# Two more attention heads transposed by VectorE and DRAM, and the plan of the late heads shifted to match, in a fused attention and two-layer feed-forward kernel

## The chip, the cores and the metric

The kernel runs on one core of one Trainium2 chip. The metric is device time in microseconds (us) of one execution, lower is better. A run is shown as the median of several executions; one further execution is recorded by the hardware profiler.

## The reference

Causal attention with a forget gate, then two feed-forward networks, all in float32:

```python
# attention: batch 4, 8 heads, 576 tokens, head width 64  (32 heads in all)
decay  = cum[..., :, None] - cum[..., None, :]       # cum = cumsum(log(clip(f)))
scores = where(causal, -1e9, q @ k.T / 8 + decay)
attn   = softmax(scores)                             # with 1e-9 in the denominator
x      = concat_heads(attn @ v)                      # 2304 tokens x 512
h = maximum(x @ w_in, 0);  x = (h * h) @ w_out       # 512 -> 2048 -> 512
h = x @ w_in2;  out = (h - tanh(h)) @ w_out2         # 512 -> 2048 -> 512
```

## The kernel before

Every operand of a product is kept as a rounded high part and a low rest, and a product is three passes on TensorE (high x high, low x high, high x low).

The first feed-forward runs in 8 blocks `j` of 288 tokens, each of 16 steps `i` over the hidden width: `h_step` (12 products `hp`, L168), then relu and two squares on ScalarE, the low part `gl` on GpSimd or VectorE, and two steps later `y_step` (12 products `yp`, L197). The 32 attention heads are worked beside these steps, so that their results are there when block `j` needs them. The second feed-forward (L1203, L1279) follows and is not touched.

There are three forms of attention work:

- `first_a` and `first_b`: heads 0 to 7, in two parts; `first_a` runs ahead of the first step and also splits the first weights of the feed-forward into high and low parts (`weights_early`, with `split_a` and `split_b`, at the head-steps that `SPLIT_A` and `SPLIT_B` give).
- `attention`: heads 8 to `UT - 1`. The softmax P is transposed by TensorE (`trans`, L549, 15 transposes a head into `t_ps`), and copied from PSUM as high (ScalarE) and low (VectorE). A generator yields after each piece; `advance` asks for pieces, so many by each half-step: 40 pieces of `first_b` and `F0` more by half-step `ENDS[0]` of block 0, the rest by half-step `ENDS[1]` of block 1.
- planned heads: `UT` to 31. P is turned in 32 x 32 blocks by VectorE (`turn`, L564 to L570), stored to DRAM (`put`, four DMAs, L574), and loaded with its blocks in their places (`get`, four DMAs into `PTl`, L580). ScalarE then makes the high part `PTh` (`p_high`), VectorE the low one (`p_low`), and `pv_begin` and `pv_end` issue the products `o_ps` (L609, L614). `plan_head` puts each of these calls into a slot; a slot is a half-step, counted from block 2 on, so that block 1 has the slots -32 to -1. Head `k` begins in slot `o = START + int(PERIOD * (k - UT - 1))`. In the blocks 2 to 5 the calls of a slot that are planned `behind` come after the step's `hp` or `yp` products, the others ahead of them.

Puts, gets, stores of x (`store_x`, L497 and L498) and loads of q, k, v and of x go through SP's queue, in the order in which they are emitted. In `pv_parts`, `out` (slot o + 7) ends with `store_x` for every second head, whose low part GpSimd makes.

The program's instructions are emitted in the order of the source. Up to the step `MARK` (block, step) the order on each engine is that of the compiler framework's scheduler; behind it, that of emission. `tc.issue_after(ins)` holds the instructions of a block behind `ins` on its engine. The letters of `ENG` name the engine of an operation (V VectorE, A ScalarE, P GpSimd, S SP's queue).

Of the kernel before, what the change touches and what calls it, by code (L numbers as in the profile page):

```python
# [16 lines left out]
B, H, S, D = 4, 8, 576, 64  # L17
# [8 lines left out]
LAG = 2  # L26
RING = 3
XLOADS = (((8, 0, 4),), ((11, 0, 3), (13, 3, 4)), ((13, 0, 4),))
F0 = 18
SLK = (None, 8)  # L30
MARK = (2, 0)
BUSY = (34, 2, 4, 6, 4, 0, 0, 0)
UT = 16
ENDS = (28, 26)
PERIOD = 7.75
START = -4
ENG = {
# [7 lines left out]
}  # L45
FETCH = {6: 4, 7: 5, 8: 6}
SPLIT_A = {4: 0, 6: 1, 8: 2, 9: 3}
SPLIT_B = {5: 0, 7: 1, 9: 2, 10: 3}
EARLY_SPLIT = 4
AHEAD_W = 3  # L50
W2EARLY = 6
TB = 288
# [17 lines left out]
def kernel(  # L70
# [31 lines left out]
    def pre(u):  # L102
        return "" if u < UT else "l_"

    def by(name):
        return {"A": nc.scalar, "V": nc.vector, "P": nc.gpsimd, "S": nc.sync}[ENG[name]]
# [15 lines left out]
    def rest(eng, out, in_, hi):  # L122
        eng.tensor_tensor(out, in_, hi.bitcast(F32), ALU.subtract)  # L123
# [15 lines left out]
    def split_a(w, i, s, stage, tag, bufs):  # L139
        raw = RAW[i][:, s]  # L140
        tmp = stage.tile([128, 2, 512], F32, tag=tag, bufs=bufs, name="wst")
        x, t = tmp[:, 0], tmp[:, 1]
        if w.dtype == I64:
            raw = raw.rearrange("p (n c) -> p n c", c=2)
            tu = t.bitcast(U32)
            nc.scalar.activation(x, raw[:, :, 1].bitcast(F32), AF.Prelu, scale=2.0 ** -112, alpha=2.0 ** 32)
            by("w1_sh").tensor_scalar(tu, raw[:, :, 0], 29, None, ALU.logical_shift_right)
            nc.vector.scalar_tensor_tensor(tu, x.bitcast(U32), 3, tu, ALU.logical_shift_left, ALU.bitwise_or)
        else:
            rounded(nc.vector, t, raw[:, :512])  # L150
        STG[i, s] = t

    def split_b(i, s):
        t = STG.pop((i, s))
        if s == 0:
            HL[0] = slot_pool(i).tile([128, 2, 2, 512], F32R, tag=f"w{i}", name=f"w{i}")
        hl = W[1, i, s] = HL[0][:, s]
        rounded(nc.scalar, hl[:, 0], t)
        rest(by(f"w1_lo{s}"), hl[:, 1], t, hl[:, 0])
# [42 lines left out]
    two = att.enter_context(tc.tile_pool(name="two", bufs=2))  # L202
# [4 lines left out]
    R, QA, QB, VR, VH, ST, XS, P, PT = {}, {}, {}, {}, {}, {}, {}, {}, {}  # L207

    def latest(engine):
        return next(x for x in reversed(nc.cur_bb.bb.instructions) if x.engine == engine)  # L210
# [118 lines left out]
    def first(h, part):  # L329
# [76 lines left out]
        def o_step():  # L406
            ps = bank0(part, "o_ps")
            t0 = tiles[0]
            for c in ((0, 2, 3, 4, 1) if part else (0, 2, 1)):
                if c == 4:  # L410
                    nc.tensor.matmul(ps[0:64, 128:256], vr[0:64, 4], ptr[0][:, 0:128], start=False, stop=False)
                    continue
                t = max(t0, c)
                nc.tensor.matmul(ps[0:64, (t - t0) * 128:256], vr[:, c], pt[0][:, c, t - 1:t0 + 1].rearrange("p t j -> p (t j)"),  # L414
                                 start=(c == 0), stop=(c == 1))
            if not part:
                ps0 = bank0(part, "o0_ps")
                nc.tensor.matmul(ps0[0:64, 0:64], vr[0:64, 0], ptr[0][:, 0:64], start=True, stop=True)
            e = h % 2
            if e == 0:  # L420
                XS[0] = two.tile([128, S], F32, tag="xs", name="xs")
            xs = XS[0]
            rr = slice(64 * e, 64 * e + 64)
            c0 = 320 if part else 64
            rounded(by("b_xs" if part else "a_xs"), xs[rr, c0:c0 + 256], ps[0:64, 0:256])
            if not part:
                rounded(by("a_xs0"), xs[rr, 0:64], ps0[0:64, 0:64])
            if e == 1:
                if part:
                    store_x(0, h // 2, xs, 320, S)  # L430
                else:
                    rounded(nc.scalar, X[0][0][:, h // 2], xs[:, :TB])
                    rest(by("a_xl"), X[0][1][:, h // 2], xs[:, :TB], X[0][0][:, h // 2])
                    rounded(nc.scalar, XE[:, 0, h // 2].bitcast(F32R), xs[:, TB:320])
                    rest(nc.gpsimd, XE[:, 1, h // 2], xs[:, TB:320], XE[:, 0, h // 2])
                    if h == H - 1:
                        for a in range(2):
                            nc.sync.dma_start(x_d[0][:, :, a, TB:320].rearrange("k p n -> p k n"), XE[:, a])
# [316 lines left out]
    def plan(slot, f, *a, behind=False):  # L755
        PLAN.setdefault(slot, ([], []))[behind].append((f, a))

    def plan_head(k):
        o = START + int(PERIOD * (k - UT - 1))
        new, old = k < NU, k > UT  # L760
        if new:
            plan(o, s_products, k, 4, behind=True)
            plan(o + 1, s_min, k, 4)
            plan(o + 1, s_exp, k, 4)
            plan(o + 1, s_products, k, 3, behind=True)
            plan(o + 2, s_min, k, 3)
            plan(o + 2, s_exp, k, 3)
            plan(o + 2, s_products, k, 2, behind=True)
            plan(o + 2, s_products, k, 1, behind=True)
            plan(o + 3, s_min, k, 2)  # L770
            plan(o + 3, s_exp, k, 2)
            plan(o + 3, s_min, k, 1)
            plan(o + 3, s_min, k, 0)
            plan(o + 3, s_exp, k, 1)
            plan(o + 3, s_exp, k, 0)
            plan(o + 3, s_sum, k, 3, 5)
            plan(o + 3, s_norm, k, 4)
            plan(o + 3, s_norm, k, 3)
            plan(o + 4, turn, 4)
            plan(o + 4, s_sum, k, 0, 3)  # L780
            plan(o + 4, s_norm, k, 2)
            plan(o + 4, s_norm, k, 1)
            plan(o + 4, s_norm, k, 0)
            plan(o + 4, turn, 3)
        if old:
            plan(o + 4, p_high, 0)
            plan(o + 4, p_high, 1)
            plan(o + 4, p_high, 2)
            plan(o + 4, p_high, 3)
            plan(o + 4, p_low, 0)  # L790
            for c in (1, 2, 3):
                plan(o + 5, p_low, c)
            plan(o + 5, pv_begin, k - 1, behind=True)
            plan(o + 6, pv_end, k - 1, behind=True)
            plan(o + 7, lambda u: PV[u][2](), k - 1)
            plan(o + 7, lambda u: PV.pop(u)[3](), k - 1)
        if new:
            plan(o + 5, turn, 2)
            plan(o + 5, turn, 1)
            plan(o + 5, turn, 0)  # L800
            plan(o + 5, put, k)
            plan(o + 6, get, k, behind=True)
        if k == UT + 1:
            plan(o, prep_v, UT)
        if k + 1 < NU:
            if k > UT + 1:
                plan(o, load, k + 1)
            plan(o + 5, prep_hi_qk, k + 1)
            plan(o + 6, prep_copy, k + 1)
            plan(o + 6, prep_low, k + 1)  # L810
        if new:
            plan(o + 4, load_v, k)
            plan(o + 8, prep_v, k)
# [6 lines left out]
    X = {0: [f1.tile([128, NK, TB], F32R, tag="xhl", bufs=4, name="xhl") for _ in range(2)]}  # L820
    setup()

    def weights_early(h):
        if h in FETCH:
            fetch_w(w1, FETCH[h], FETCH[h])
        if h in SPLIT_B:
            for s in range(2):
                split_b(SPLIT_B[h], s)
        if h in SPLIT_A:
            for s in range(2):  # L830
                split_a(w1, SPLIT_A[h], s, two, "QA", 2)

    TA = one.tile([128, 2048], F32, tag="T", name="TA")
    XE = TA[:, 1024:1280].rearrange("p (a k n) -> p a k n", a=2, k=NK)
    first_a(weights_early)

    def w1_ahead(i):
        if EARLY_SPLIT <= i + AHEAD_W - 1 < NF:
# [21 lines left out]
    def advance(to):  # L860
        while cnt[0] < min(to, total):
            next(ga, None)
            PEI[cnt[0]] = latest(EngineType.PE)
            cnt[0] += 1
# [232 lines left out]
    later = []  # L1097
    for k in range(UT + 1, NU + 1):
        plan_head(k)
    for g in range(NB * NF + LAG):  # L1100
        j, i = divmod(g, NF)
        if (j, i) == MARK:
# [330 lines left out]
    for n in range(REST):  # L1433
        k, g = divmod(n, NG)
# [103 lines left out]
```

## Time and profile before

| | |
|---|---|
| median of 3 runs | 1002.09 us (1002.01 to 1003.88) |
| the profiled execution, its own time | 1002.52 us |
| its span, first to last instruction | 1000.7 us |
| TensorE busy, products and weight loads | 978.0 and 930.1 us |
| VectorE, ScalarE, GpSimd busy | 722.6, 615.8, 393.7 us |
| mean granted TensorE clock | 0.994 |

The span is what the views of the trace divide; what lies between it and the execution's own time is outside all instructions. Products overlap in the records, each is listed with its whole passage, so the distance between two starts tells what one costs. The steps of block 0 start at 48.9 us, of block 1 at 164.8, of block 2 at 262.6, of block 3 at 329.4, of block 4 at 395.9, of block 5 at 462.7, of block 6 at 523.2 and of block 7 at 574.3 us.

### The profile page before, as it was taken

The page shows a single profiled execution, that of the slowest core. Times are in us where ns is not written, and L with a number is a line of the kernel's source. Part 1 is how long each engine was busy: PE and PEld are TensorE (multiplying, and loading weights), DVE is VectorE, ACT ScalarE, POOL GpSimd, SP SyncE. Part 2 cuts the span into 40 slices and gives each one's busy share as a digit, 9 for nine tenths or more (in the row PEclk, how much of TensorE's full clock was granted, in tenths as well). Part 3 has the DMA queues.
Part 4 walks back from the last instruction along what each step waited for, and adds up shares of the span by engine and source line. Part 5 has one row for each costly group of instructions (what it writes and reads, how often), then busy time and mean ns, then how long its engine had stood idle before and what let it go on. Part 6 is the DMA issues. An engine that isn't in the chain of part 4 may idle for free.

```text
span 1000.7 us, 19994 instructions
## 1 busy us (share of the span) xinstructions
PE 978.0 (98%) x7144; PEld 930.1 (93%) x7144; DVE 722.6 (72%) x1715; ACT 615.8 (62%) x1387; POOL 393.7 (39%) x452
## 2 busy tenths in 40 slices
PE   7989999999999999999999999999999999999998
PEld 6767778888999999999999999999999999999998
DVE  5998774777676878778626577567878787887851
ACT  5988786766686777777657777455566553333330
POOL 4343565455454435454304547146657520000000
PEclk8999999999999999999999999999999999999999
DMA  8646551223657576766547984987776798434351
GB/s 259 256 129 207 174 164 65 92 83 122 202 204 251 205 235 221 248 217 225 195 161 265 348 284 175 396 335 265 273 269 240 252 349 330 148 117 137 127 169 64
DMA packets 91443, 211.56 MB, mean 211 GB/s; under 512 B 9208, under 2 KB 33840, under 8 KB 89040
## 3 DMA queue, kind: packets, MB, share of 16 engines
q1 hardware_dynamic: 91216, 210.29, 60.7%
q8 instruction: 56, 0.92, 0.4%
q14 instruction: 43, 0.35, 0.1%
q10 hardware_dynamic: 128, 0.01, 0.0%
HBM read 132.20 MB, written 78.05 MB: 210 GB/s over the span
## 4 chain that ended last, share of the span: by engine, by line
PE 82%; DVE 6%; DMA 5%; ACT 3%; issue 1%; POOL 1%; SPq 1%; DVEq 0%; POOLq 0%; ACTq 0%
PE yp L197 19%; PE hp L168 19%; PE wp L1279 16%; PE wp L1203 12%; PE o_ps L609 4%; PE wp L1291 2%; DMA g_d<-gq 2%; PE o_ps L414 2%; PE s_ps L373 1%; PE s_ps L702 1%; DVE wt L973 1%; PE s_ps L701 1%; PE t_ps L549 1%; DMA R<-in_qk_dram 1%; PE t_ps L395 1%
## 5 line engine op out<-in xcount | busy, mean ns | idle before, releaser
L168 PE MATMUL hp<-xhl,w 128*128 128x288 f32 x1536 | 234.6, 298 | 3.5 <-ACT xhl L110 1.6
L168 PEld LDWEIGHTS hp<-xhl,w 128*128 128x128 f32 x1536 | 212.6, 189 | 6.8 <-ACT xhl L110 1.8
L197 PE MATMUL yp<-gh,w 128*128 128x288 f32 x1024 | 213.1, 299 | 0.0
L197 PEld LDWEIGHTS yp<-gh,w 128*128 128x128 f32 x1024 | 165.1, 189 | 1.9 <-issue 1.3
L1203 PE MATMUL wp<-xo,wg 128*128 128x288 f32 x1152 | 160.2, 296 | 2.9 <-DVE gq L1210 2.7
L1279 PE MATMUL wp<-go,wg 128*128 128x256 f32 x1344 | 161.4, 283 | 0.0
L1279 PEld LDWEIGHTS wp<-go,wg 128*128 128x128 f32 x1344 | 161.4, 192 | 0.0
L1203 PEld LDWEIGHTS wp<-xo,wg 128*128 128x128 f32 x1152 | 155.5, 189 | 4.2 <-DVE gq L1210 4.1
L197 PE MATMUL yp<-gl,w 128*128 128x288 f32 x512 | 152.2, 297 | 0.6 <-POOL gl L123 0.6
L525 POOL TENSOR_SCALAR P<-P,ST 128x192 f32<-128x192 f32 (+4 forms) x120 | 96.6, 812 | 134.7 <-DVE ST L717 79.3
L110 ACT ACTIVATE go<-gt 128x1792 fp32r<-128x1792 f32 (+1 forms) x34 | 58.3, 1717 | 101.4 <-PE wp L1279 73.3
L514 ACT ACTIVATE P<-P,ST 128x320 f32<-128x320 f32 (+4 forms) x151 | 84.8, 562 | 38.2 <-DVE ST L505 37.8
L505 DVE CUSTOM_DVE_ANT_0 P<-s_ps,mk 128x320 f32<-128x320 f32 (+3 forms) x151 | 63.3, 436 | 61.2 <-PE s_ps L702 33.3
L123 DVE TENSOR_TENSOR gl<-tmp,gh 128x288 fp32r<-128x288 f32 x96 | 60.1, 627 | 53.2 <-ACT tmp L178 52.7
L197 PEld LDWEIGHTS yp<-gl,w 128*128 128x128 f32 x512 | 96.7, 189 | 1.2 <-POOL gl L123 0.8
L123 DVE TENSOR_TENSOR go<-gt,go 128x1792 fp32r<-128x1792 f32 (+1 forms) x34 | 69.6, 2047 | 35.4 <-ACT go L110 32.3
L174 ACT ACTIVATE tmp<-hp 128x288 f32<-128x288 f32 x128 | 51.7, 404 | 58.6 <-PE hp L168 56.5
L123 POOL TENSOR_TENSOR wt<-wt,whi 128x512 f32<-128x512 f32 (+1 forms) x48 | 60.6, 1283 | 59.2 <-ACT whi L110 27.6
L178 ACT ACTIVATE tmp<-tmp 128x288 f32<-128x288 f32 x128 | 56.7, 443 | 3.3
L177 ACT ACTIVATE gh<-tmp 128x288 fp32r<-128x288 f32 x128 | 56.1, 438 | 2.0
L1210 DVE TENSOR_TENSOR gq<-wp,sm 128x288 f32<-128x288 f32 x96 | 40.7, 452 | 17.6 <-ACT sm L1209 10.7
L1341 POOL TENSOR_TENSOR gq<-sm,sm 128x288 f32<-128x288 f32 x32 | 28.6, 893 | 56.0 <-ACT sm L1340 34.8
(167 smaller groups left out, 1720.3 us busy)
## 6 DMA issues: line engine op xcount, KB each, us to landing
wg<-wg_d SPq DMA_DIRECT2D x24, 896.0 KB
g_d<-gq SPq DMA_DIRECT2D x32, 576.0 KB
raw<-in_w_dram SPq DMA_DIRECT2D x16, 1024.0 KB
p_d<-T SPq DMA_DIRECT2D x64, 256.0 KB
PTl<-p_d SPq DMA_DIRECT2D x64, 256.0 KB
raw<-in_w_dram SPq DMA_DIRECT2D x32, 512.0 KB
gt<-g_d SPq DMA_DIRECT2D x32, 512.0 KB
R<-in_qk_dram SPq DMA_DIRECT2D x24, 576.0 KB
```

Source lines behind the costliest of these rows:

```text
L110: eng.activation(out, in_, AF.Copy)
L123: eng.tensor_tensor(out, in_, hi.bitcast(F32), ALU.subtract)
L168: nc.tensor.matmul(ps, w[:, k * 128:(k + 1) * 128], x[:, k], start=(jj == 0), stop=(jj == 11))
L174: nc.scalar.activation(tmp, ps, AF.Relu)
L177: nc.scalar.activation(gh, tmp, AF.Square)
L178: nc.scalar.activation(tmp, tmp, AF.Square)
L197: nc.tensor.matmul(yp[m][:, :n], w[:, c], x, start=(at == 0 and j == 0), stop=(at == NF - 1 and j == 2))
L505: nc.vector.tensor_tensor_reduce(p[:rows, a:b], ps[:rows, :b - a], mk[:rows, o:o + b - a], -0.125, 3.0e38 if mn is None else mn, ALU.add, ...
L514: nc.scalar.activation(p[:rows, :n], p[:rows, :n], AF.Exp, bias=mn, scale=-1.0, accum_out=st[:rows, 1, t:t + 1])
L525: by(n_by).tensor_scalar(p[:rows, :n], p[:rows, :n], st[:rows, 3, t:t + 1], 1.0, ALU.mult, ALU.mult)
L1203: nc.tensor.matmul(ps, wg[:, ws, k * 128:(k + 1) * 128], xo[:, xs, k], start=(i == 0 and first_), stop=(i == 5), skip_group_check=True)
L1279: nc.tensor.matmul(ps, wg[:, ws, m * 128:(m + 1) * 128], YO[n][xs][:, YX[xn]], start=(j == 0 and m == 0 and i == 0), stop=(j == 2 and i == ...
```

## The change

`UT` goes from 16 to 14: heads 14 and 15 leave `attention` and become planned heads. The plan starts at slot -20 instead of -4, now with head 15 (16 slots are two periods of 7.75 and a half). So block 0 takes 26 pieces beyond the 40 instead of 18, and block 1 the remaining 32 by half-step 13 instead of 58 by half-step 26. `MARK` moves to block 1, step 10. The loads `get` go from slot o + 6, behind, to slot o + 7, and there they stand behind `out` and its `store_x`. In the opening, the split of weight 3 moves one head-step later, its instructions of the last two head-steps are held behind ScalarE's latest instruction, and the low part of the last pair of x goes from GpSimd to VectorE (`a_xe`). Two pieces of `first_b` are asked for ahead of the first step.

```diff
-F0 = 18
+F0 = 26
-MARK = (2, 0)
+MARK = (1, 10)
-UT = 16
-ENDS = (28, 26)
+UT = 14
+ENDS = (28, 13)
-START = -4
+START = -20
     "a_xl": "P",
+    "a_xe": "V",
-SPLIT_A = {4: 0, 6: 1, 8: 2, 9: 3}
-SPLIT_B = {5: 0, 7: 1, 9: 2, 10: 3}
+SPLIT_A = {4: 0, 6: 1, 8: 2, 10: 3}
+SPLIT_B = {5: 0, 7: 1, 9: 2, 11: 3}
-  rest(by("a_xl"), X[0][1][:, h // 2], xs[:, :TB], X[0][0][:, h // 2])
+  rest(by("a_xl" if h < H - 1 else "a_xe"), X[0][1][:, h // 2], xs[:, :TB], X[0][0][:, h // 2])
             plan(o + 5, put, k)
-            plan(o + 6, get, k, behind=True)
+            plan(o + 7, get, k)
     def weights_early(h):
         if h in FETCH:
             fetch_w(w1, FETCH[h], FETCH[h])
+        with tc.issue_after(latest(EngineType.Activation)) if h == H + 2 else ExitStack():
             (split_b and split_a of SPLIT_B and SPLIT_A, as before)
     first_a(weights_early)
+    with tc.issue_after(latest(EngineType.Activation)):
+        weights_early(H + 3)
     for k in range(UT + 1, NU + 1):
         plan_head(k)
+    advance(2)
```

## Rows read from the trace of the kernel before

**Rows 1.** The table of stretches: length, busy us (instructions) of each engine, clock, DMA.

```profile
48.90:164.80 115.90, 108.73 (x641) 84.80 (x640) 90.32 (x246) 89.76 (x210) 56.86 (x76) 0.99 0.49 155
164.80:262.60 97.80, 97.33 (x658) 86.92 (x657) 67.21 (x228) 64.68 (x171) 52.30 (x72) 1.00 0.33 110
...
329.40:395.90 66.50, 66.50 (x491) 65.37 (x490) 54.51 (x142) 49.37 (x123) 32.04 (x37) 1.00 0.64 216
...
523.20:574.30 51.10, 51.10 (x385) 51.10 (x385) 31.68 (x58) 36.55 (x81) 24.00 (x20) 1.00 0.83 299
```

**Rows 2.** Waits of TensorE: us in total, times, longest.

```profile
PE hp L168 <- ACT xhl L110: 1.6, 1, 1.6
PE hp L168 <- DMA xhl<-x_d: 0.8, 1, 0.8
PE hp L168 <- POOL xhl L123: 0.6, 1, 0.6
```

**Rows 3.** The stretches again, products on o_ps alone (PE first).

```profile
164.80:262.60 97.80, 21.90 (x91) 13.32 (x91) 6.20 (x14) 4.17 (x7) 1.00 0.33 110
...
329.40:395.90 66.50, 9.48 (x57) 8.60 (x57) 3.25 (x8) 2.38 (x4) 1.00 0.64 216
```

**Rows 4.** Timeline of TensorE, block 1: start, us, engine, line, operation.

```profile
205.44 0.60 PE L549 MATMUL t_ps<-ident,P 128*128 128x128 f32 x4
205.80 0.45 PE L538 MATMUL s_ps<-QA 128*128 128x448 f32 x1
...
208.91 0.74 PE L609 MATMUL o_ps<-PTh,VH 128*128 128x512 f32 x2
...
210.01 0.40 PE L168 MATMUL hp<-xhl,w 128*128 128x288 f32 x1
...
212.25 1.34 PE L168 MATMUL hp<-xhl,w 128*128 128x288 f32 x9
```

**Rows 5.** Timeline of TensorE, block 3.

```profile
345.81 0.97 PE L609 MATMUL o_ps<-PTh,VH 128*128 128x512 f32 x5
346.62 1.82 PE L168 MATMUL hp<-xhl,w 128*128 128x288 f32 x12
348.27 1.03 PE L609 MATMUL o_ps<-PTl,VH 128*128 128x512 f32 x5
...
349.28 0.52 PE L197 MATMUL yp<-gh,w 128*128 128x288 f32 x2
```

**Rows 6.** Block 3, VectorE's turns at L567 alone.

```profile
329.40:395.90 66.50, 9.39 (x17) 1.00 0.64 216
```

**Rows 7.** Timeline of all engines, opening, around the first step's input.

```profile
51.77 1.22 ACT L146 ACTIVATE wst<-raw 128x512 f32<-128x512 f32 x2
...
52.90 0.43 ACT L110 ACTIVATE xhl<-xs 128x288 fp32r<-128x288 f32 x1
...
53.40 1.01 POOL L123 TENSOR_TENSOR xhl<-xs,xhl 128x288 fp32r<-128x288 f32 x1 [4.74 <-ACT xhl L110]
```

**Rows 8.** Timeline of all engines around head 20.

```profile
319.50 3.06 SPq L580 DMA_DIRECT2D PTl<-p_d  x4
...
320.39 1.44 POOL L123 TENSOR_TENSOR xs<-xs,xsh 128x576 f32<-128x576 f32 x1 [0.64 <-ACT xsh L110]
...
328.26 2.08 ACT L110 ACTIVATE PTh<-PTl 128x512 fp32r<-128x512 f32 x4
...
331.00 0.80 PE L609 MATMUL o_ps<-PTh,VH 128*128 128x512 f32 x3
```

**Rows 9.** Tile p_d: DMA issues, ns min/median/max, first and last start.

```profile
L574 SPq DMA_DIRECT2D p_d<-T x64: 319/434/1042, 252.7 to 494.4; - x64
L580 SPq DMA_DIRECT2D PTl<-p_d x64: 577/582/792, 257.2 to 497.3; - x64
```

**Rows 10.** Tile PTl: ScalarE's copies, first and last start; who waited.

```profile
L110 ACT ACTIVATE PTh<-PTl x64: 507/617/636, 264.4 to 503.4; 128x512 fp32r<-128x512 f32 x48, 128x384 fp32r<-128x384 f32 x16
...
ACT PTh L110: 1.3, 2
```

More of the change, by code (lines that the diff above doesn't have):

```diff
@@ L825, in weights_early @@
             fetch_w(w1, FETCH[h], FETCH[h])
[L826 to L831, printed above, removed]
+        with tc.issue_after(latest(EngineType.Activation)) if h == H + 2 else ExitStack():
+            if h in SPLIT_B:
+                for s in range(2):
+                    split_b(SPLIT_B[h], s)
+            if h in SPLIT_A:
+                for s in range(2):
+                    split_a(w1, SPLIT_A[h], s, two, "QA", 2)
     TA = one.tile([128, 2048], F32, tag="T", name="TA")
```

2 rows, old and new, of the table ENG are left out of this document.

## The prediction

> **What bounds the kernel now.** I read the table of stretches first: TensorE is busy for the whole of every stretch behind the opening, 97.33 of 97.80 us and 66.50 of 66.50, at a granted clock of 1.00, which is the 2.4 GHz level [rows 1]. So from about 50 us on the time is the sum of TensorE's products, and an edit changes the time only by what it adds to or takes from that sum, or by a wait that it puts into it. The waits of TensorE come next: the longest that this change touches are those ahead of the first hp product of the first feed-forward, 1.6 us for ScalarE's and 0.6 us for GpSimd's part of the input, and 0.8 us at 264 us for a load of x [rows 2]. Third, what one head costs TensorE. The stretch from 523.20 has a block of 16 steps without heads: 51.1 us. The same 16 steps take 97.8 us where the heads are transposed by TensorE, and 66.5 us where VectorE and DRAM turn them [rows 1]. The reader is to see that the excess is the heads: 46.7 us for 91 o_ps products, which at 13 a head are 7.0 heads, so 6.67 us a head; and 15.4 us for 57 products, 4.4 heads, so 3.5 us a head [rows 1, 3].
>
> **Two heads change their kind.** By blocks the difference is 6.67 - 3.5 = 3.17 us a head, 6.3 us for two. By pieces, from starts to starts: four transposes take 205.80 - 205.44 = 0.36 us, 0.09 us each, and a head has 15, so 1.35 us. Its o_ps products run from 208.91 to 212.25, less one hp product from 210.01, which costs 51.1 / 384 = 0.13 us in the block without heads: 3.21 us [rows 1, 4]. A turned head's take 346.62 - 345.81 = 0.81 and 349.28 - 348.27 = 1.01 us, 1.82 together [rows 5]. So 1.35 + 1.39 = 2.74 us a head, 5.5 us for two, to which the blocks add the scores, which run closer together in the later form. Nothing on TensorE is added: scores and products are as many in either form. I take **-6.3** (the whole blocks leave nothing out) with -5.5 as the poor end.
>
> **What the two heads cost elsewhere.** VectorE turns: 17 turns of L567 take 9.39 us in a stretch with four heads, about 2.4 us a head [rows 6]; the small pieces come on top. What covers it is VectorE's free time: it is busy 67.21 of 97.80 us in the block that gets them, and 54.51 of 66.50 us where this is done already [rows 1], and TensorE doesn't wait there. Cost nothing; were that cover gone, 2 x 2.4 = +4.8. ScalarE's four copies a head replace four others of the same size: nothing. Eight more puts and eight more loads go through SP's queue in a block whose DMA share is 0.33 [rows 1]: nothing, apart from the order, below.
>
> A rule of the Trainium skill speaks against the edit. VectorE's L567 takes 9.39 / 17 = 0.55 us for a turn that TensorE does as three or four transposes at 0.09 us [rows 4, 6]: TensorE is the faster of the two here, too. The Trainium skill, VectorE: DVE Perf Modes, section Rules for kernel authors, advises TensorE for a 128 x 128 transpose if the result may go to PSUM. By that the edit should lose about 2 x (2.4 - 1.35) = 2.1 us; by the rows it gains, because the engine that is relieved is the full one.
>
> **The opening.** Before the last pair's high copy (xhl, ScalarE, at 52.90 us) stand two widening steps of a weight, 1.22 us from 51.77; the low copy follows on GpSimd from 53.40 and takes 1.01 us [rows 7]. This weight is the one whose split is moved a head-step later and queued behind ScalarE's last copy. Without them the high copy starts 1.1 us earlier, and on VectorE the low copy should take about half of GpSimd's 1.01 us (the page has no such tile on VectorE there): 1.1 + 0.4 = **-1.5**. The poor end is 0: VectorE and ScalarE are busy 90.32 and 89.76 of 115.90 us in this stretch [rows 1], the split's work is not less, and what the first step gains may be waited for a few steps later. The good end is -2.2, both waits gone [rows 2], with the two pieces of the next heads that now stand ahead of the first step filling what is left. What is late next if the split comes late is the fourth step's weight, and there TensorE would wait.
>
> The denser first block (66 pieces of heads by its end where 58 were) moves work between blocks, not into the sum: 0, the cover being VectorE's and ScalarE's remaining fifth [rows 1].
>
> **The load behind the store.** In the later blocks SP issues the four loads of turned values before the two stores of an even-odd pair; by the new place in the plan it does so behind them, and the second store waits for GpSimd's low part. For head 20 the loads went at 319.50 and took 3.06 us; GpSimd's xs ends at 320.39 + 1.44 = 321.83, and the store takes SP some 0.4 us more, so the loads go 2.8 us later, end issuing at 325.4 [rows 8]. How long the landing takes is bounded by the last head: its last load goes at 497.3, its fourth copy starts at 503.4, so (three copies of 0.62 before) its first at 501.5 and no wait: 3.6 us or less from the end of the issue [rows 9, 10]. So head 20's values come by 329.0, its copies start 0.7 us after 328.26, and the fourth ends at 331.1; TensorE asks for the fourth product 0.8 us after 331.00 [rows 8]. No wait, with 0.7 us to spare. Over 16 heads ScalarE waited for these loads only twice, 1.3 us in all [rows 10]. There are seven such heads. Poor end: every load lands just in time today, and the whole 2.8 us less TensorE's cover of 1.46 us (331.80 less 328.26 + 2.08) is paid seven times, +9.4; good end 0. The rows stand near the good end: **+1.0**. Behind the loads on SP are the next head's q, k and v, which are needed a head later.
>
> **The seam.** Today the heads' pieces end at half-step 26 of the second block (slot -7) and the copies of the first turned head stand at slot 0; after the edit they end at half-step 13 (slot -20) and the copies of head 14 stand at slot -16, four half-steps on. From the first put at 252.7 to the first copy at 264.4, which waited for its load, 11.7 us went by [rows 9, 10]. Four half-steps at the pace of turned heads are 4 x 66.5 / 32 = 8.3 us [rows 1]. So ScalarE would wait 3.4 us at head 14's copies; TensorE asks for them a half-step later, 2.1 us of cover, and the scheduler may place them later. **+1.4**, from 0 to +3.4. Queued behind these copies are ScalarE's relu and squares, and the next hp product waits for the relu. The wait for x at the start of the third block (0.8 us) stays: head 15's store comes at slot -6, with six half-steps to go as now; at best the 0.8 us go.
>
> **Sum.** -6.3 - 1.5 + 1.0 + 1.4 = -5.4. The profiled execution took 1002.5 us, so 997.1; the median of the runs stands 0.4 us below that execution, so **996.7 us**.
>
> **Rivals.**
> 1. No new wait, opening in full: -6.3 - 2.2 - 0.8 = -9.3, 992.8 us. For it: the later blocks have no wait at all on TensorE. Against it: 3.4 us are missing for head 14.
> 2. The gain is lost at the seams: heads by pieces (-5.5), nothing at the opening, seam +3.4, load +1.0: -1.1, 1001.0 us.
> 3. The load behind the store is late in all seven heads, the other sign: +9.4 against -6.3 - 1.5 + 1.4, so +3.0, 1005 us. It decides from (6.3 + 1.5 - 1.4) / 7 = 0.9 us of TensorE's wait per such head. For it: the shift of 2.8 us is certain by the order of SP's queue. Against it: two short waits in 16 heads.
> 4. VectorE's turns aren't covered: the block becomes VectorE's and the 6.3 us come back as waits: -1.5 + 1.0 + 1.4 = +0.9, 1003 us, and up to 4.8 more. Against it: VectorE has 30 us free there [rows 1]. By the advice of the page cited above a loss of this kind is the outcome to expect.
>
> **How the numbers follow.** My forecast holds with 0.57 (994.5 to 999 us), rival 1 with 0.19, rival 2 with 0.12, rival 3 with 0.08, rival 4 with 0.04. The range from 992.8 to 1001.3 takes in the forecast, rivals 1 and 2: 0.88, less what lies at its ends, some 0.8. About 0.2% (2 us) is what a measurement of this kernel can tell. Faster by that is below 1000.1 us: the forecast, rival 1 and a third of rival 2, 0.80. Within it: the rest of rival 2 and most of rival 4, 0.11. Slower: rival 3 and the rest of rival 4, 0.09.
>
> **What would show it.** In the profile after, t_ps has 30 products fewer; the second block is shorter by about twice 3 us, and the blocks behind it are as long as now. The ScalarE wait at the first hp product falls below 0.6 us. Waits of o_ps for PTh sum to about 1 us in the later blocks and to about 1.4 us near the middle of the second block. It is wrong if TensorE's waits for PTh or for the loads reach 6 us, or if hp waits for a weight at the fourth step.

## The result, and the profile after

| | before | after |
|---|---|---|
| median of the runs | 1002.74 us (1002.01 to 1003.88, 4 runs) | 1014.55 us (1011.64 to 1015.46, 4 runs) |
| profiled execution, its span | 1002.52, 1000.7 us | 1015.46, 1013.7 us |

The ratio is 1.0112, 95% interval 1.0092 to 1.0132: 12 us slower, where 996.7 us was forecast and 1001.3 was the end of the range. The sign was wrong.

The table of stretches after, blocks 0 to 4 and the block without heads (columns as in [rows 1]):

```profile
47.80:169.80 122.00, 114.70 (x677) 88.56 (x676) 95.94 (x278) 96.70 (x227) 62.68 (x84) 1.00 0.52 167
169.80:262.90 93.10, 90.53 (x591) 81.24 (x591) 59.36 (x194) 58.80 (x149) 48.08 (x63) 0.96 0.41 137
262.90:338.30 75.40, 71.50 (x492) 67.00 (x490) 51.49 (x143) 51.66 (x130) 31.61 (x39) 0.98 0.63 209
338.30:405.50 67.20, 67.19 (x494) 65.44 (x493) 53.55 (x144) 50.35 (x123) 30.50 (x36) 1.00 0.64 217
405.50:475.90 70.40, 69.28 (x489) 66.27 (x488) 51.04 (x140) 49.31 (x123) 29.98 (x36) 0.98 0.62 214
...
536.20:587.40 51.20, 51.20 (x387) 51.20 (x385) 31.73 (x58) 36.64 (x81) 24.01 (x20) 1.00 0.80 293
```

Eight pieces of heads moved from block 1 to block 0, so these two are read together: 215.1 us against 213.7 before [rows 1]. Block 2 takes 75.4 us where it took 329.4 - 262.6 = 66.8, block 4 takes 70.4 where it took 462.7 - 395.9 = 66.8; block 3 takes 67.2 us for 66.5, and the block without heads 51.2 for 51.1. So blocks 2 and 4, which the forecast left at their length but for short waits, lose 12.2 us, and the first two blocks don't gain. The granted clock is 0.98 in blocks 2 and 4, 0.96 in block 1, and 1.00 in the others shown.

TensorE's waits after (us in total, times, longest), as [rows 2]:

```profile
PE o_ps L609 <- ACT PTh L110: 2.9, 3, 1.3
...
PE hp L168 <- DMA xhl<-x_d: 1.7, 2, 1.0
PE o_ps L609 <- issue: 1.5, 3, 1.1
...
PE hp L168 <- ACT xhl L110: 0.6, 1, 0.6
```

And tile PTl after, as [rows 9, 10]: the loads and ScalarE's copies, and in the last line how long an engine that uses the tile sat idle until a load of it landed (us, times). All 11 are ScalarE, ahead of the first copy of a head:

```profile
L580 SPq DMA_DIRECT2D PTl<-p_d x72: 577/583/1295, 223.0 to 510.7; - x72
L110 ACT ACTIVATE PTh<-PTl x72: 505/616/637, 230.4 to 516.2; 128x512 fp32r<-128x512 f32 x54, 128x384 fp32r<-128x384 f32 x18
...
  DMA PTl<-p_d: 16.8, 11
```

The opening's waits fell as forecast: for the high part from 1.6 to 0.6 us, and the one for GpSimd's low part is gone. The last line above is where the time went. ScalarE waited 1.3 us in 2 of 16 heads for turned values [rows 10]; now it waits 16.8 us in 11 of 18. TensorE's waits look small beside that, and one head shows why. Timeline after, all engines, around head 26:

```profile
420.58 1.79 SPq L574 DMA_DIRECT2D p_d<-T  x4
...
425.96 0.32 SPq L498 DMA_DIRECT2D x_d<-xs  x1
426.39 2.55 SPq L580 DMA_DIRECT2D PTl<-p_d  x4
428.98 0.59 SPq L273 DMA_DIRECT2D R<-in_qk_dram  x1
429.61 0.34 SPq L275 DMA_DIRECT2D QB<-aug_d  x1
...
430.05 0.57 SPq L294 DMA_DIRECT2D VR<-in_v_dram  x1
...
435.35 2.09 ACT L110 ACTIVATE PTh<-PTl 128x512 fp32r<-128x512 f32 x4 [3.09 <-DMA PTl<-p_d]
436.07 1.86 PE L609 MATMUL o_ps<-PTh,VH 128*128 128x512 f32 x5 [1.08 <-issue]
437.77 0.48 PE L197 MATMUL yp<-gh,w 128*128 128x288 f32 x2
...
440.40 1.58 PE L609 MATMUL o_ps<-PTl,VH 128*128 128x512 f32 x5
```

The same head before:

```profile
412.12 1.79 SPq L574 DMA_DIRECT2D p_d<-T  x4
414.33 2.96 SPq L580 DMA_DIRECT2D PTl<-p_d  x4
...
417.97 0.42 SPq L498 DMA_DIRECT2D x_d<-xs  x1
418.44 0.44 SPq L273 DMA_DIRECT2D R<-in_qk_dram  x1
...
423.76 2.08 ACT L110 ACTIVATE PTh<-PTl 128x512 fp32r<-128x512 f32 x4
426.44 0.98 PE L609 MATMUL o_ps<-PTh,VH 128*128 128x512 f32 x5
```

Before, the loads came first and ScalarE didn't wait. After, they stand behind the second store, end issuing at 428.94, and the first copy waits until 435.35: they landed 6.4 us after the end of their issue. What this costs TensorE at this head has three parts. It idles 1.08 us. Then its five products run as fast as ScalarE makes their operands: they take 437.77 - 436.07 = 1.70 us where they took 0.81 [rows 5], and since their records overlap, the page counts this as busy. Third, the clock falls, as the table of stretches after shows around that place (PEclk is the third column from the end):

```profile
437.00:439.00 2.00, 1.98 (x11) 1.71 (x11) 2.00 (x5) 1.97 (x5) 0.00 (x0) 0.79 0.00 0
439.00:441.00 2.00, 2.00 (x9) 1.90 (x9) 1.76 (x4) 1.48 (x4) 1.62 (x2) 0.50 0.43 158
441.00:443.00 2.00, 2.00 (x16) 1.90 (x15) 0.30 (x1) 0.60 (x1) 1.11 (x2) 0.86 0.98 367
```

From 439 to 441 us it is 0.50, the 1.2 GHz level. The twelve yp products from 437.77 to 440.40 take 2.63 us; at the pace of the block without heads they take 12 x 51.1 / 384 = 1.60 [rows 1]. The five products behind them take 441.82 - 440.40 = 1.42 us instead of 1.01 [rows 5]. So 1.08 + 0.89 + 1.03 + 0.41 = 3.4 us, of the 3.6 that block 4 lost.

The clock doesn't fall at each late head. At head 19 TensorE idles longer, its products are paced alike, and the granted clock stays at 1.00:

```profile
318.53 1.81 PE L609 MATMUL o_ps<-PTh,VH 128*128 128x512 f32 x5 [1.33 <-ACT PTh L110]
320.19 1.85 PE L168 MATMUL hp<-xhl,w 128*128 128x288 f32 x12
...
320.00:322.00 2.00, 2.00 (x15) 2.00 (x16) 2.00 (x6) 1.97 (x4) 0.71 (x2) 1.00 0.00 0
```

In block 2 it falls elsewhere, behind TensorE's two waits for x (the 1.7 us above, at 264.9 and 266.5 us; 0.8 us before [rows 2]). The load of x stands directly behind head 16's turned loads, as it did before:

```profile
257.94 2.94 SPq L580 DMA_DIRECT2D PTl<-p_d  x4
260.92 1.06 SPq L894 DMA_DIRECT2D xhl<-x_d  x2
...
269.00:271.00 2.00, 2.00 (x10) 1.91 (x9) 0.76 (x1) 1.17 (x3) 1.93 (x2) 0.52 0.72 268
```

In the first of the experiments below 4.4 us lie between the end of the one issue and the other, and TensorE doesn't wait for x. So a part of block 2's loss is this wait and the clock behind it, not late copies; it wasn't tested apart.

### The profile page after: what moved, and what is told of

Read it like the earlier page. It is cut to its first block, busy times and chain, and to the rows that moved or that the text cites. A ratio compares the mean times of both kernels' runs of the same rounds, so it can differ in the third digit from the quotient of the medians.

```text
span 1013.7 us, 19946 instructions
## 1 busy us (share of the span) xinstructions
PE 985.3 (97%) x7114; PEld 930.9 (92%) x7114; DVE 717.1 (71%) x1712; ACT 618.8 (61%) x1385; POOL 388.0 (38%) x453
## 4 chain that ended last, share of the span: by engine, by line
PE 72%; DMA 9%; DVE 8%; ACT 5%; issue 3%; POOL 2%; SPq 1%; DVEq 0%; ACTq 0%; POOLq 0%
PE wp L1283 16%; PE yp L197 16%; PE hp L168 15%; PE wp L1207 11%; PE o_ps L609 4%; DMA PTl<-p_d 2%; PE wp L1295 2%; DMA g_d<-gq 2%; DMA R<-in_qk_dram 2%; PE o_ps L414 1%; DVE wt L976 1%; PE s_ps L373 1%; POOL QB L123 1%; PE s_ps L702 1%; PE s_ps L701 1%
## 5 line engine op out<-in xcount | busy, mean ns | idle before, releaser
L197 PE MATMUL yp<-gh,w 128*128 128x288 f32 x1024 | 216.7, 302 | 0.0
L197 PEld LDWEIGHTS yp<-gh,w 128*128 128x128 f32 x1024 | 167.7, 191 | 1.6 <-issue 1.2
L525 POOL TENSOR_SCALAR P<-P,ST 128x192 f32<-128x192 f32 (+4 forms) x118 | 87.0, 748 | 116.6 <-DVE ST L717 79.5
L123 DVE TENSOR_TENSOR PTl<-PTl,PTh 128x512 fp32r<-128x512 f32 x72 | 45.0, 675 | 18.0 <-ACT PTh L110 17.9
```

The source lines that it names most:

```text
L197: nc.tensor.matmul(yp[m][:, :n], w[:, c], x, start=(at == 0 and j == 0), stop=(at == NF - 1 and j == 2))
L525: by(n_by).tensor_scalar(p[:rows, :n], p[:rows, :n], st[:rows, 3, t:t + 1], 1.0, ALU.mult, ALU.mult)
```

## The experiments

Each run has the kernel before as its partner on the same chip; ratios are to that partner, with a 95% interval.

**The place of the loads, undone and alone.** `e1_loads_back` is the changed kernel with the loads in their old place; `e2_loads_alone` is the kernel before with the loads in the new one.

```diff
# e1, from after                              e2, from before: the reverse
-            plan(o + 7, get, k)
+            plan(o + 6, get, k, behind=True)
```

> The changed kernel with the four loads of turned values back in slot o + 6, behind, ahead of the stores on SP's queue; all else as changed. Theory A (the loads behind the store are what costs): the blocks 2 to 5 go back to 66.8, 66.5, 66.8 and 60.5 us from 75.4, 67.2, 70.4 and 60.3, about 13 us less, so 1000 to 1004 us, and ScalarE's waits for the loads fall from about 2 us each at heads 18, 19, 20, 24, 26 and 28 to under 1 us. Theory B (the seam in block 1 and the denser block 0 cost it, the later blocks only carry the shift): 1011 to 1015 us.

> The kernel before with one edit alone, the loads of turned values in slot o + 7 behind the stores. Theory A: 8 to 13 us slower than before, 1010 to 1015 us, with ScalarE waiting 2 to 3 us for the loads at the heads that follow a store, and TensorE's clock at its lower level for some us behind at least one of these waits. Theory B: within 2 us of before.

e1: 1006.49 us, 1.0036 (1.0015 to 1.0057). e2: 1012.7 us, 1.0077 (1.0048 to 1.0107). So the one moved line costs 7 to 8 us, in either kernel; ScalarE waits 12.3 us in 9 heads for turned values in e2, and 6.8 us in 4 in e1. It is most of the loss, but e1 is still slower than before. The stretches of e1, blocks 1 to 4:

```profile
168.80:259.20 90.40, 87.83 (x592) 78.52 (x592) 59.01 (x194) 58.75 (x150) 48.42 (x63) 1.00 0.43 146
259.20:329.80 70.60, 69.51 (x492) 65.54 (x490) 52.66 (x143) 51.62 (x130) 32.31 (x39) 1.00 0.65 217
329.80:396.60 66.80, 66.80 (x495) 65.61 (x493) 53.56 (x144) 49.98 (x123) 33.67 (x37) 1.00 0.64 220
396.60:462.30 65.70, 65.70 (x488) 64.66 (x486) 52.96 (x142) 48.80 (x122) 31.87 (x36) 1.00 0.68 230
```

Blocks 3 and 4 are whole again, and the clock is 1.00; what is left is in blocks 1 and 2.

**The slot, or the store?** `e4_loads_first` keeps the loads in slot o + 7, ahead of `out`.

```diff
+            if new:
+                plan(o + 7, get, k)
             plan(o + 7, lambda u: PV[u][2](), k - 1)
             plan(o + 7, lambda u: PV.pop(u)[3](), k - 1)
...
-            plan(o + 7, get, k)
```

> The changed kernel with the loads of turned values still in slot o + 7, but emitted there ahead of the products' eviction and so ahead of the store. It tells the place behind the store from the slot. Theory A as I hold it (the store's wait for GpSimd on SP's queue is the cause): as with the loads in slot o + 6, 1000 to 1004 us. Theory A2 (the slot itself is too late): 1008 us or more.

1005.78 us, 1.0028 (1.0011 to 1.0045), ScalarE's waits for turned values 6.6 us in 4 heads: as e1. It is the place behind the store.

**The opening, undone and alone.** `e3_opening_back` undoes the opening's edits (`SPLIT_A`, `SPLIT_B`, `a_xe`, the two held splits, `advance(2)`) in the changed kernel, and `e5_opening_alone` makes them in the kernel before.

```diff
-SPLIT_A = {4: 0, 6: 1, 8: 2, 10: 3}
+SPLIT_A = {4: 0, 6: 1, 8: 2, 9: 3}
...
-    advance(2)
```

> The changed kernel with the opening as before: weight 3 split where it was, the last low copy on GpSimd, no pieces ahead of the first step. Theory A: the opening gave 1 to 2 us, so 1015 to 1017 us. Theory C (the opening's edits cost time in block 0, which now takes 122.0 us for 115.9): 1008 to 1013 us.

> The kernel before with the opening's edits alone (weight 3 split a head-step later and behind ScalarE's last copy, the last low copy on VectorE, two pieces ahead of the first step). As I predicted it: 1.5 us faster than before, 1000.5 to 1002 us, the first step's wait for ScalarE below 0.6 us. Rival (VectorE, nearly full in the first half of block 0, takes it back): within 0.5 us of before.

e3: 1015.49 us, 1.0104 (1.0070 to 1.0137), the changed kernel's own 1.0112 within its interval. e5: 1005.53 us, 1.0014 (0.9995 to 1.0033). TensorE's waits for the last pair of the first input are 0.6 us in e5 and 1.6 and 0.6 us, as before, in e3; no gain is seen in the time.

**The order in block 1.** There the planned calls of a slot came after the `hp` step and its relu and squares, where blocks 2 to 5 put them between. `e6_order_block1` is e1 with that order from `MARK` on. `e7_puts_ahead` is e6 with head 14's puts ahead of head 13's products and store.

```diff
-            if 2 <= j < NB - 2:
+            if 2 <= j < NB - 2 or (j == 1 and i >= MARK[1]):
...
-            if j == 1:
+            if j == 1 and i < MARK[1]:
```

> The changed kernel with the loads of turned values back in slot o + 6 (as in the first experiment), and in block 1 from step 10 on the planned calls placed as in the later blocks, so ahead of the step's relu and squares on ScalarE and not behind them. Theory S1 (in block 1 the copies of heads 15 and 16 and the exponentials stand behind relu and squares, which wait for hp, and TensorE waits for them): the first five products of heads 15 and 16 fall from 1.69 to 0.82 us each, TensorE's wait of 0.9 us for scores at 251 us goes, and the run takes 2 to 4 us less than the first experiment's 1006.5. Theory S2 (the loads land late there, whatever ScalarE's order): no change.

> The one before (loads in slot o + 6, block 1 in the later blocks' order) with the turns and the four puts of head 14 emitted ahead of head 13's products and store, so that the puts don't stand behind that store on SP's queue. Theory S3 (head 14's late values are the store's doing: its puts were issued from 217.0 to 222.5 us around two stores): ScalarE's wait of 2.0 us at head 14's copies falls below 0.5 us and the run is 1 to 3 us faster than the one before it. Rival (four half-steps are too few anyhow): ScalarE still waits over 1 us.

e6: 1003.35 us, 0.9998 (0.9981 to 1.0015), block 1 three us shorter than in e1:

```profile
172.50:259.90 87.40, 86.61 (x593) 78.43 (x592) 60.01 (x197) 60.01 (x155) 48.75 (x64) 1.00 0.46 155
259.90:329.70 69.80, 67.97 (x492) 65.50 (x490) 53.82 (x141) 50.21 (x124) 33.06 (x38) 1.00 0.65 215
```

e7: 1003.23 us, 0.9991 (0.9972 to 1.0010), and ScalarE still waits 2.1 us at head 14: puts ahead of that store alone don't bring its values sooner. Its loads still stand behind the store there (226.36 us, behind 225.93), so the store isn't cleared by this run.

**Head 19's short distance.** What stayed in e6's block 2 was one wait, 2.7 us on ScalarE, at head 19, whose successor starts seven slots on instead of eight. `e9_gap_at_18` moves the short distance to head 18, `e11_gap_at_20` starts head 20 alone a slot later, and `e10_ends_11` is e11 with head 14's pieces ended two half-steps sooner.

```diff
-        o = START + int(PERIOD * (k - UT - 1))
+        o = START + int(PERIOD * (k - UT - 1) - 0.25)       # e9
+        o = START + int(PERIOD * (k - UT - 1)) + (k == UT + 6)       # e11, e10
...
-ENDS = (28, 13)
+ENDS = (28, 11)       # e10
```

> e6_order_block1 with the 7-slot distance moved from head 19 to head 18 (and from 23, 27 and 31 to 22, 26 and 30). What is left in e6 in block 2 is one wait: ScalarE 2.7 us at head 19's copies, TensorE 1.1 us and five products of 1.66 us instead of 0.82, so some 2 us. If the short distance between head 19 and 20 makes it (G1), the wait at head 19 falls by about a half-step (2.1 us) to under 0.8 us, head 18 gets one of under 1 us, the blocks from 262 us on are as before (66 to 67 us each), and the time is 1.5 to 2 us under e6, 1001.5 on its scale. If it is the load of x on SP ahead of head 19's loads (G2), the wait stays over 1.5 us and the time is e6's.

> e6_order_block1 with head 20's start alone one slot later (19 instead of 18, as in the kernel before), so that eight slots lie between 19 and 20, and seven between 20 and 21. G1: head 19's wait falls from 2.7 to about 0.6 us on ScalarE and to 0 on TensorE, head 20 waits under 1 us; 1.5 to 2 us under e6. G2: as e6, with 2 us or more of wait at head 19.

> e11_gap_at_20 with head 14's pieces ended two half-steps sooner (half-step 11 of the second block instead of 13), its copies where they were. The seam's theory: head 14 has four half-steps between its last piece and its copies, two too few; with six ScalarE's wait there falls from 1.4 us to under 0.3, its first five products take 0.82 us again, and the time is 1 us or so below e11. Rival: the pieces pressed into fewer half-steps of block 1 only make ScalarE or VectorE late there, and the time is e11's or 1 us over it. If both this and the distance hold, the time is 1.5 to 3 us under the kernel before.

e9: 1001.25 us, 0.9990 (0.9969 to 1.0011). e11: 1001.84 us, 0.9988 (0.9969 to 1.0008). e10: 1001.22 us, 0.9986 (0.9971 to 1.0002). The distance was the cause: head 19's wait goes to nothing in e9 and to 1.2 us in e11 (1.4 in e10), and head 18 gets none. In e10 head 14's wait goes from 1.8 to 0 us, and no gain is seen in the time: block 0 takes 123.2 us instead of 121.2 in e11, block 1 87.9 instead of 88.9. Block 0's granted clock is 0.97 in e10 and 1.00 in e11, so its 2.0 us don't tell what the pieces cost there. The stretches of e9, blocks 1 and 2:

```profile
169.00:257.90 88.90, 87.58 (x593) 78.52 (x592) 59.46 (x197) 60.03 (x156) 47.79 (x64) 1.00 0.45 151
257.90:325.90 68.00, 66.92 (x491) 65.33 (x490) 53.81 (x142) 50.46 (x124) 35.81 (x38) 1.00 0.68 222
```

`e12_best_opening_back` is e9 with the old opening.

> e9_gap_at_18 with the opening as in the kernel before: what is left of the change is the two heads, their place, and the three repairs (loads ahead of the store, the order in block 1, the distance moved). If the opening is worth nothing, as e3 and e5 say, the time is e9's within 1.5 us, 0.998 to 1.000 of before. If it costs the 1.4 us that e5 had as its middle, 0.9975 of before, clearly faster. If it gains the 1.5 us that was predicted, 1.0005 of before.

1003.63 us, 0.9991 (0.9975 to 1.0008): e9's ratio, though a difference of 1.5 us is within the two intervals.

**Why the landing took 6.4 us.** In the changed kernel the loads of heads 30 and 31, behind which no q and k go, landed 3.6 and 3.3 us after the end of their issue (behind head 30's went its v). Those of heads 18, 20, 24, 26 and 28, with the next head's q and k directly behind, took 5.5, 5.2, 4.8, 6.4 and 5.3 us, and head 19's, with a load of x directly ahead as well, 7.0. Head 22 is the exception, 3.7 us with q and k as close:

```profile
361.86 2.87 SPq L580 DMA_DIRECT2D PTl<-p_d  x4
364.76 0.66 SPq L273 DMA_DIRECT2D R<-in_qk_dram  x1
...
368.39 2.09 ACT L110 ACTIVATE PTh<-PTl 128x512 fp32r<-128x512 f32 x4 [0.33 <-DMA PTl<-p_d]
```

Four runs tried to take these followers away: `e8_qkv_later` puts them a slot later, `e13_next_loads_off` and `e14_loads_behind_copies` hold them behind ScalarE's work by `issue_after`, and `e15_next_loads_held` by a write of VectorE into their buffer, which SP must wait for.

```diff
-                plan(o, load, k + 1)
+                plan(o + 1, load, k + 1)              # e8
+                plan(o + 3, load_late, k + 1)         # e13; e14: in o + 4, behind the first copy
+                plan(o + 3, load, k + 1, True)        # e15
...
+        if hold:                                      # e15, in load
+            nc.vector.memset(R[u][:, 0, :1], 0.0)
```

> The changed kernel (loads of turned values behind the store) with the load of the next head's q and k one slot later. In the changed kernel the turned values were copied 6.4 us after the issue of their last load had ended (head 26), twice what I had counted, while q and k of the next head were already being moved. Theory L1 (q and k, right behind on SP's queue, stretch the landing): ScalarE's waits at heads 18, 19, 20, 24, 26 and 28 fall by 1 to 3 us each and the run takes 3 to 8 us less than 1014.5. Theory L2 (only the time of issue counts): no change.

> The changed kernel, with the next head's q and k (and behind them v) held on SP until ScalarE has reached the step ahead of the copies, so that they no longer follow the four turned loads directly (in e8_qkv_later they still did: 434.0 us behind loads that ended at 434.0). In the changed kernel the loads of heads 30 and 31, which have no q and k behind them, landed 3.6 and 3.3 us after their issue, those of heads 18 to 28 that ScalarE waited for 3.7 to 7.1 us. A1, the next head's loads share the transfer with them: all land in under 4 us, ScalarE's waits at heads 18, 19, 20, 24, 26 and 28 (1.2 to 3.1 us) fall by 1.5 to 2.5 us each, blocks 2 and 4 are 3 us or more shorter together, and the time is 3 to 5 us under the changed kernel (1.006 to 1.008 of before) unless q and k come late for their own use. A2, the two stores ahead make the landing long: waits and time as in the changed kernel, within 1.5 us.

> The changed kernel, with the next head's q and k loads held on SP until ScalarE has made its first copy of the turned values, which is behind their landing (in e13_next_loads_off the hold was set where ScalarE had already passed it, and in most heads the loads still followed at once), and their splitting a slot later. A1, the next loads share the transfer: the turned loads of heads 18 to 28 land 3.3 to 4 us after the end of their issue instead of 4.8 to 7.1, ScalarE's waits there fall by 1.2 us or more each. A2, the two stores ahead: the landing stays at 5 us and more and the waits are as in the changed kernel. The time says less, since q and k themselves now come 6 us later, and ScalarE may wait for them: 1008 to 1016 us.

> The changed kernel with the next head's q and k loads held by a real dependence: VectorE writes one column of their buffer behind its norms of the head, so that SP can't issue them before (e13 and e14 only gave the order a hint, and in most heads that waited the loads still followed the turned ones at once). They should go some 2.7 us later: at 431.6 instead of 429.0 on the changed kernel's scale of head 26. A1, the next loads share the transfer: the turned loads of heads 18, 19, 20, 24, 26, 28 land in under 4.5 us after the end of their issue instead of 4.8 to 7.1, ScalarE's wait at 26 falls from 3.1 us to under 1.5 us and the six together from 12 us to under 6 us; time 3 us or more under the changed kernel. A2, the two stores ahead: landing and waits as in the changed kernel within 0.5 us a head.

e8: 1017.56 us, 1.0138 (1.0113 to 1.0164). e13: 1015.66 us, 1.0123 (1.0096 to 1.0149). e14: 1044.99 us, 1.0424 (1.0392 to 1.0456). None of the three did what it was for. A slot only orders SP's queue, and `issue_after(ins)` holds what goes on the engine of `ins`: that is ScalarE here, while these loads are SP's. So in e8's head 26, in most heads of e13 that show a wait, and in e14's heads 19 and 26, q and k still went within 0.1 us of the turned loads. e14 lost its 42 us elsewhere, half of it shown by one row: its products of scores waited 21.9 us for GpSimd, in eight waits; the splitting of q and k had moved a slot, but whether that is why wasn't tested. From e8 I had read that the followers don't matter; that reading was wrong.

e15: 1007.72 us, 1.0046 (1.0016 to 1.0076), by the ratios 6.6 us under the changed kernel, with the loads still behind the store. Its head 26:

```profile
422.79 0.32 SPq L500 DMA_DIRECT2D x_d<-xs  x1
423.21 2.56 SPq L582 DMA_DIRECT2D PTl<-p_d  x4
428.40 0.34 SPq L275 DMA_DIRECT2D R<-in_qk_dram  x1
...
429.25 2.09 ACT L110 ACTIVATE PTh<-PTl 128x512 fp32r<-128x512 f32 x4 [0.23 <-DMA PTl<-p_d]
...
431.59 0.98 PE L611 MATMUL o_ps<-PTh,VH 128*128 128x512 f32 x5
```

q and k go 2.6 us later, and the turned values land 429.25 - 425.77 = 3.5 us after the end of their issue, not 6.4. At heads 18, 20 and 28 it is 3.3, 3.4 and 3.6 instead of 5.5, 5.2 and 5.3. Heads 19 and 24, which have a load of x beside them in the queue, still wait 2.5 and 2.9 us; head 24 waits longer than the 1.2 us of the changed kernel. Over heads 18, 19, 20, 24, 26 and 28 the waits fall from 13.1 to 6.7 us, where under 6 was expected. The store ahead costs the loads their start; at these four heads (18, 20, 26, 28) the loads behind cost them their landing. Why head 22 lands soon with or without them is open.

The Trainium skill, DMA: Bandwidth & Descriptors, section Queues, rings and completion order, says that each DMA engine takes descriptors in ring order, and goes on that a later one may still finish its write before an earlier one. By the first half alone one would not expect what stands behind a load to delay it; the second half leaves room for it. With the followers held back, the four landings named came 1.7 to 2.9 us sooner (e15).

**All repairs.** `e16_all_repairs` is e9 with the hold of e15.

> e9_gap_at_18 (loads ahead of the store, planned order in the second block, short distance at 18) with the next head's q and k held as in e15. If what is left of ScalarE's waits for turned loads in e9 (4.3 us in 5, 2.2 us of it ahead of a copy of theirs) is the same sharing, it falls under 3 us and the time is 0.5 to 1.5 us under e9, 0.998 of before; if the heads' copies there are early enough anyhow, as the short waits behind block 2 say, the time is e9's, 0.999 of before, and the hold only brings a risk of late q and k (0 to 1 us more).

1005.40 us, 1.0029 (1.0010 to 1.0048): slower than e9's 0.9990, the two intervals just touching. With the loads ahead of the store nothing is seen to be won, and q and k now come late themselves: ScalarE waits up to 3.6 us for them, and block 3 takes 69.0 us instead of 66.8.

## Why the prediction was wrong, step by step

- **The load behind the store (+1.0, range to +9.4): the step that failed.** It measured 7.6 to 7.7: 7.7 alone on the kernel before (e2, 4.8 to 10.7), 7.6 of the changed kernel's 11.2 when undone (e1, from the two ratios). The shift of 2.8 us was sized a little short (the loads start 426.39 - 420.58 = 5.8 us behind the first put at head 26, 2.2 before). What failed is the landing. "3.6 us or less" was read from head 31, the one head with no next head, so with nothing behind its loads; the sentence on q, k and v asked only when they are needed, not what they do to the loads ahead. e15 shows that with q and k 2.1 to 2.6 us behind it is 3.3 to 3.6 us at other heads, too (18, 20, 26 and 28). By its ratio e15, with the loads still behind the store, stands 1.0 us from e1 (1.0046 and 1.0036, within the intervals), so the +1.0 fits the shift alone. The poor end of the step was near the truth, the value taken was not, and the row that decided between them was the least like the rest.

Two readings behind the step were off as well. The row of products in [rows 8] ends inside its group, with three of five; the fourth starts at 331.64, which leaves 0.5 us to spare instead of 0.7, and a cover of 1.3 us instead of 1.46. And head 31's copies stand closer together than 0.62 us, so the first starts 501.88 - 497.92 = 4.0 us after the end of the issue:

```profile
331.64 0.34 PE L609 MATMUL o_ps<-PTh,VH 128*128 128x256 f32 x2
...
501.88 2.07 ACT L110 ACTIVATE PTh<-PTl 128x512 fp32r<-128x512 f32 x4
```

With both, 0.2 us is left, and the poor end comes to 7 x (2.8 - 1.3) = +10.5.

- **Rival 3** is what happened, with 0.08. Its threshold, 0.9 us of TensorE's wait a head, was too simple: late copies also pace the five products (0.9 us), and at head 26 the clock fell behind them (1.4 us). For the same reason the sign that was to show the forecast wrong, 6 us of TensorE's waits, didn't show: the page has 2.9 us for PTh and 1.5 for `issue`.
- **The seam (+1.4, to +3.4): under-sized.** ScalarE waits 2.0 us at head 14, where 3.4 were reckoned. (The 11.7 us they were reckoned from don't end with a wait for the load: the trace puts head 16's 1.1 us before to `issue`, and the two load waits of [rows 10] are those of heads 19 and 21.) But the planned calls in block 1 came behind relu and squares in ScalarE's queue, and so behind `hp` products; that cost 3 us (e1 to e6). This was in the code, and the forecast named the queue, but only in the other direction. Head 19's distance added about 2 us of block 2 in the profiles, which the times (e6 to e9) don't resolve. The wait for x, which was to stay at 0.8 us, rose to 1.7.
- **Two heads change their kind (-6.3): held in mechanism, short in size.** t_ps has 30 products fewer, and from start to next start t_ps costs 19.52 us before and 16.51 after in the first two blocks. With the other losses out, these blocks take 257.9 - 48.2 = 209.7 us in e9, 208.5 in e6, 210.1 to 211.1 in e10 to e12 and 213.0 in e7, so 0.7 to 5.2 less than the 213.7 before, with late copies of ScalarE still in them. That VectorE's turns are covered nearly stands, too: in block 1 the waits that VectorE ended sum to 1.3 us after (none before), not to rival 4's 6.3. So for TensorE's own cost the advice of the Trainium skill that is cited there (VectorE: DVE Perf Modes, Rules for kernel authors) isn't borne out where TensorE is the full engine; in the time of the whole kernel the gain isn't clear of zero.
- **The opening (-1.5): no gain**, its own poor end: e5's interval leaves at most 0.5 us of it. In e5 the first step starts at 48.9 us, as before, and the first two blocks take 214.3 us where they took 213.7. The waits for the first input are down to 0.6 us in e5 and back at 1.6 and 0.6 in e3, so the edit does what it says, and the 1.6 us are spent again within the two blocks; where, wasn't taken apart. The changed kernel's own first step starts at 47.8 us, 1.1 sooner, but that goes with the clock: e3, with the old opening, starts it at 47.9, and both have a granted clock of 0.96 up to there. Before and in e5 (48.9 us each) it is 0.93, in e6 (51.4 us) 0.90. Starts of the first step can't be compared between profiles without it.
- **Sum.** In ratios, from the changed kernel to e9: 11.2 us, less 7.6 for the loads, 3.8 for the order, 0.8 for the distance, leaves -1.0 us (-3.1 to +1.1). The five best versions (e7, e9 to e12) stand at 0.9986 to 0.9991, none with an interval clear of 1. Without the term of the loads the sum was -6.4; e9's profile shows 470.9 us for blocks 0 to 5 where it was 474.3, so -3.4; but its profiled execution, 998.73 us, is 2.5 us under its median, so the ratio is the better measure. Of the 3.0 us between -6.4 and -3.4, 1.5 are the opening. ScalarE's waits at heads 14 and 15 (1.8 us each in e9) and block 2 (68.0 us for 66.8) can hold the rest; they weren't taken apart.

## What to carry to other kernels

A landing time belongs to the loads that share its place in the queue: take it from a row with the same neighbours ahead and behind, never from the last of a series. When a load is moved in a queue, ask three things: what it now waits behind, what now follows it, and whether the engine that uses it works just in time; at head 26 a copy late by 3.1 us cost the full engine 3.4 us, although 1.3 to 1.5 us of it had been reckoned as covered. And a busy full engine may be paced: compare the start-to-start time of a group with an undisturbed one before believing that it doesn't wait.

## What the runs showed of the hardware that was not expected

- On one queue, four loads of 256 KB landed 3.3 to 3.6 us after the end of their issue where no q and k followed within 2 us (heads 30 and 31; heads 18, 20, 26 and 28 in e15), and 4.8 to 6.4 us at five heads with the next head's q, k and v directly behind. It isn't a rule: at head 22 it was 3.7 us with them directly behind.
- After a wait of a microsecond TensorE could be at half its clock: behind 1.08 us idle and five products of 0.34 us each at head 26 the granted clock was 0.50 from 439 to 441 us. After 1.33 us idle and products paced alike at head 19 it was 1.00. In the blocks of e1, e6 and e9 shown above it is 1.00, although e1's waits of ScalarE at heads 14 and 19 are 2.0 and 2.7 us.
- One and the same kernel spreads more than its first four runs say: the kernel before, 1002.0 to 1003.9 us in its first four, gave 997.8 to 1009.0 us over all chips, the 12 runs of e9 997.9 to 1007.3. A change of 1 us is out of reach of 12 runs.
